# Two softmaxes of a batch: all keys and all queries in one TensorE visit each, with their spare columns in mm1's banks

## The chip, the cores and the metric

The kernel runs on one core of a Trainium2 chip. Its time is the device time of one execution in microseconds (us); a comparison takes the median of several executions. The profile of one further execution gives the start and duration of every instruction. The engines are called PE (TensorE, matmuls; PEld its weight loads), DVE (VectorE), ACT (ScalarE), POOL (GpSimd) and SP (SyncE, which issues most of the DMAs). Each takes its instructions in the order in which the program has them.

## The reference

Per batch (8) and head (8), 32 packed queries `p` attend to 576 keys and values, and then the 576 queries `q` attend to the 32 packed rows. Two feed-forward layers follow, the second with one of eight experts per token.

```python
def sm_attn(qq, kk, vv):
    s = scale * np.matmul(qq, kk.transpose(0, 1, 3, 2))
    s = s - np.max(s, axis=-1, keepdims=True)
    a = np.exp(s)
    a = a / (np.sum(a, axis=-1, keepdims=True) + 1e-09)
    return np.matmul(a, vv)
p_packed = sm_attn(p, k, v)
out = sm_attn(q, p_packed, p_packed)
...
h = x @ w_in                       # _moe_ref, 4608 tokens, 512 -> 2048 -> 512
g = h * (1.0 / (1.0 + np.exp(-h)))
return (g @ w_out).astype(np.float32)
...
e_idx = np.argmax(logits, axis=1)  # _moe2_ref, the chosen one of 8 experts
h = np.maximum(x[mask] @ w1[e], 0.0)
out[mask] = gate_w[mask, None] * eom[mask, e, None] * (h @ w2[e])
```

## The kernel before

The order of the work is written out by hand. `batch(b)` runs 16 steps f for each of the 8 batches. In a step PE does mm1 (12 matmuls of 288 columns into `ps_h`: the first feed-forward product for 128 hidden columns and the batch's 576 tokens) and then mm2 of two steps before (12 matmuls of 512 columns into four accumulators). Between them ACT applies tanh to `ps_h` (L728), DVE multiplies tanh plus one by `ps_h` into g (L729, the product), and ACT and DVE split g into a high and a low part (L734, L739; L746, L748 for the last 64 tokens). In odd batches step 1 has 48 further matmuls in mm2 at the end of the batch before.

PSUM has eight banks: four accumulators, two for `ps_h`, and two for `ps_a`, which serves everything else. There is one buffer of each, so mm1 of a step waits until the product of the step before has read `ps_h`.

Beside the steps of batch b, `extra_steps` places the attention of batch b + 1 as nine small steps s1 to s9, at a step f and a position: position 0 is behind mm1, tanh and product, position 1 behind mm2. For b of 1 to 6:

- s1(h), h of 0 and 1, at (0, 1) and (3, 1): `tiles8` multiplies half of the keys by p. It issues 8 matmuls of 64 rows by 32 columns of weights, four heads by two rows of heads, each over 288 columns of a half (L579). DVE takes the maximum (L594), ACT copies the scores to e (L595); after the second half ACT takes the exponential (L601), queued in `late` and so issued in step 4.
- s2(r) at (4, 1) and (5, 1): PE transposes e (L609), ACT copies it out.
- s3 at (7, 1): PE multiplies by the values (L627), and the same visit holds the logits of the batch before (L324). DVE normalizes into pp (L632).
- s4 at (8, 1): PE turns pp and the logits; ACT copies ppt (L642); DVE sums the logits and finds the expert (L343, then `finish`, L794 to L797).
- s5(h) at (9, 1) and (12, 1): the queries of half h times ppt (L579), DVE transposes the scores (L659) and takes the maximum.
- s6, s7, s8, s9 by half: subtract and exponential; sum, reciprocal and scaling (L671 to L675); transpose back and high part; low part. s7(0) is at (10, 1), s8(0) and s9(0) at (11, 1), s7(1) at (13, 1), s8(1) and s9(1) at (14, 1).

`step_m` (8 matmuls of 512 columns, L579 with `ps_m`) comes in steps 2, 6, 10 and 14. `place` counts the tokens of each expert for the batch before (L824, 14 or 20 small matmuls) in step 11; four blocks of rows belong to it in odd batches, five in even ones; `put` then scatters them from POOL. Loads go out on SP's queue: k1 in step 0, q0 in step 3, v1 in step 5, q1 in step 9, and p, k0, v0 of the batch after in step 13. Batch 7 has no attention beside it.

Of the kernel before, what the change touches and what calls it, by code (L numbers as in the profile page):

```python
# [84 lines left out]
class Kernel:  # L85
# [10 lines left out]
    def run(self):  # L96
# [23 lines left out]
        self.flip = False  # L120
# [432 lines left out]
    def load_att(self, b, what, dst=None):  # L553
        nc, pa = self.nc, self.pa
        n, h = what[0], int(what[1:] or 0)
        if n == "p":
            src, shape = self.i["p"][b], [128, 4, NP]
        elif n == "v":
            src, shape = self.i["v"][b, h], [128, 5, 256]
        else:  # L560
            src, shape = self.i[n][b, :, :, h * HS:h * HS + HS], [128, 4, HS]
        if what == "v1" and b > 1:
            t = self.rt.tile([128, 5, DM], F32, tag="xr", name="att_v1").rearrange("p a b -> p (a b)")[:, :1280].rearrange("p (a b) -> p a b", a=5)
# [17 lines left out]
    def att_steps(self, b):  # L581
# [4 lines left out]
        def s1(h):  # L586
# [9 lines left out]
            if h == 1:  # L596
# [56 lines left out]
        def s5(h):  # L653
# [15 lines left out]
        def s7(h):  # L669
# [4 lines left out]
            eng = nc.gpsimd if b == 1 or b == h == 0 else nc.vector  # L674
            eng.tensor_tensor(out=grp(x), in0=grp(x), in1=per_token(mx[:, 1, :]), op=ALU.mult)  # L675

        def s8(h):
            y = pa.tile([128, 2, HS], F32, tag="ea", name="y2") if b or not h else self.y_first
            nc.vector.transpose(out=y.rearrange("p a b -> p (a b)"), in_=st["x"][h].rearrange("p a b -> p (a b)"))
            nc.scalar.copy(out=self.a2[b % 2][0][:, :, h * HS:h * HS + HS], in_=y)  # L680
            st["y"][h] = y

        def s9(h):
            hi, lo = [t[:, :, h * HS:h * HS + HS] for t in self.a2[b % 2]]
# [22 lines left out]
    def mm1(self, b, f):  # L707
# [433 lines left out]
```

## Time and profile before

| | us |
|---|---|
| median of three runs | 1199.94 (1199.8 to 1200.64) |
| the profiled execution | 1199.41 |
| its span, first to last instruction | 1197.6 |
| PE busy | 1148.9 (96%) |
| DVE busy | 653.6 (55%) |
| ACT busy | 463.6 (39%) |
| batches 1 to 6 in the span | 139.75 to 674.50 |

The mean granted clock of PE is 0.988. Busy time is a mean over parts with different limits; batches 1 to 6 have to be read by themselves. In the timeline a row is a run of like instructions of one engine: start, length from the first's start to the last's end, what it is, how many, and in brackets the engine's idle time before it and what ended that. The matmuls overlap, so a length is not a price: the price of something on PE is what it adds between the start of one mm1 and the start of the next.

### The profile page before, as it was taken

Reading aid. Unit: us, or ns where it says so; the run is one execution under the profiler, and the core shown is the slowest. Engines: PE = TensorE matmul, PEld = TensorE weight load, DVE = VectorE, ACT = ScalarE, POOL = GpSimd, SP = SyncE. Lnnn points to the kernel's source line nnn. Section 1 sums busy time; section 2 is a strip of 40 time slices with the busy share of each in tenths; the row PEclk is TensorE's granted clock in tenths of the full one; section 3 lists DMA queues with packets and bytes.
Section 4 is the critical chain, followed back from the end, with each engine's and each line's share of the span. In section 5 each row is a group of like instructions: output and inputs, shape, how many; then the busy total and the mean of one; then the engine's idle time right before and its main releaser. Section 6 shows DMA issues by size and latency. Waiting matters only on the chain. (4 is left out here: it accounts for less than half of the span.)

```text
span 1197.6 us, 19835 instructions
## 1 busy us (share of the span) xinstructions
PE 1148.9 (96%) x7859; PEld 951.8 (79%) x7859; DVE 653.6 (55%) x1327; ACT 463.6 (39%) x885; POOL 170.7 (14%) x178
## 2 busy tenths in 40 slices
PE   6688999999999999999999999999999999999996
PEld 3465777877877877777877888789999998998995
DVE  6988646546656446646446656354445454454531
ACT  3343443343443343443343434234343343434331
POOL 0224300000100000100000121033121303211021
PEclk8898999999999999999999999999999999999999
DMA  9565240240241230231230153145554636445211
GB/s 330 179 201 190 70 113 24 98 95 23 69 108 26 96 95 24 85 92 37 84 96 21 38 130 92 45 141 165 171 156 130 196 100 193 132 150 167 89 58 42
DMA packets 105286, 130.28 MB, mean 109 GB/s; under 512 B 13888, under 2 KB 80640, under 8 KB 104928
## 3 DMA queue, kind: packets, MB, share of 16 engines
q1 hardware_dynamic: 97888, 108.83, 30.7%
q0 software_dynamic: 7296, 20.09, 5.1%
q8 instruction: 64, 1.05, 0.4%
q14 instruction: 38, 0.31, 0.1%
HBM read 99.19 MB, written 21.57 MB: 101 GB/s over the span
## 5 line engine op out<-in xcount | busy, mean ns | idle before, releaser
L770 PE MATMUL acc<-wo,ghi 128*128 128x512 f32 x1024 | 318.4, 392 | 0.0
L719 PE MATMUL ps_h<-a,mb 128*128 128x288 f32 x1536 | 235.4, 303 | 14.6 <-DVE g L729 8.0
L719 PEld LDWEIGHTS ps_h<-a,mb 128*128 128x128 f32 x1536 | 215.8, 192 | 40.0 <-DVE g L729 15.8
L770 PEld LDWEIGHTS acc<-wo,ghi 128*128 128x128 f32 x1024 | 192.7, 188 | 37.2
L1055 PE MATMUL pu<-xt,w 128*128 128x256 f32 (+1 forms) x1536 | 214.6, 295 | 0.2
L1055 PEld LDWEIGHTS pu<-xt,w 128*128 128x128 f32 x1536 | 208.4, 189 | 6.1 <-issue 0.8
L770 PE MATMUL acc<-wo,glo 128*128 128x512 f32 x512 | 204.4, 399 | 0.0
L1080 PE MATMUL py<-w,xt 128*128 128x512 f32 x768 | 188.2, 394 | 0.0
L1080 PEld LDWEIGHTS py<-w,xt 128*128 128x128 f32 x768 | 144.2, 188 | 33.4
L729 DVE SCALAR_TENSOR_TENSOR g<-g,ps_h 128x576 f32<-128x576 f32 x128 | 96.1, 750 | 118.2 <-ACT g L728 118.2
L1061 DVE SCALAR_TENSOR_TENSOR xt<-pu,xt 128x512 fp32r<-128x512 f32 (+1 forms) x128 | 58.7, 458 | 156.2 <-ACT xt L1060 150.2
L1060 ACT ACTIVATE xt<-pu 128x512 fp32r<-128x512 f32 (+1 forms) x128 | 52.6, 411 | 222.7 <-PE pu L1055 163.5
L728 ACT ACTIVATE g<-ps_h 128x576 f32<-128x576 f32 x128 | 83.3, 651 | 142.1 <-PE ps_h L719 134.7
L770 PEld LDWEIGHTS acc<-wo,glo 128*128 128x128 f32 x512 | 96.6, 189 | 42.8 <-issue 20.5
L739 DVE TENSOR_TENSOR glo<-g,ghi 128x512 fp32r<-128x512 f32 x128 | 91.3, 713 | 60.1 <-ACT ghi L734 59.5
L841 POOL DMA_INDIRECT perm<-pay,dsti x36 | 35.2, 979 | 575.0 <-DVE dsti L839 512.7
L734 ACT CAST ghi<-g 128x512 fp32r<-128x512 f32 x128 | 79.4, 620 | 87.8 <-DVE g L729 86.7
L1017 DVE TENSOR_TENSOR w<-raw,w 128x1024 fp32r<-128x1024 f32 x64 | 78.3, 1225 | 43.1 <-ACT w L1016 28.9
L1016 ACT CAST w<-raw 128x1024 fp32r<-128x1024 f32 x64 | 66.9, 1047 | 0.0
L700 DVE TENSOR_TENSOR mb<-ps_m,mb 128x1024 fp32r<-128x1024 f32 (+1 forms) x35 | 39.1, 1117 | 19.0 <-ACT mb L696 18.7
L770 PE MATMUL accL<-wo,gl 128*128 128x512 f32 x192 | 46.0, 394 | 0.0
L1097 POOL DMA_INDIRECT out<-y,xix x32 | 39.3, 1228 | 46.8 <-ACT y L1089 37.7
(189 smaller groups left out, 918.1 us busy)
## 6 DMA issues: line engine op xcount, KB each, us to landing
raw<-in_w SPq DMA_DIRECT2D x64, 512.0 KB
att_v<-in_v SPq DMA_DIRECT2D x15, 640.0 KB
att_k<-in_k SPq DMA_DIRECT2D x15, 576.0 KB
stg<-in_w_in SPq DMA_DIRECT2D x16, 512.0 KB
stg<-in_w_out SPq DMA_DIRECT2D x16, 512.0 KB
xr<-xr SPq DMA_DIRECT2D x32, 256.0 KB
att_q<-in_q SPq DMA_DIRECT2D x14, 576.0 KB
mid<-xr SPq DMA_DIRECT2D x28, 256.0 KB
```

The lines of the kernel that those rows point to most:

```text
L719: nc.tensor.matmul(ps[:, hf, :288], lw[:, qd, fs], rx[:, qd, ts], start=(i == 0), stop=(i == 5))
L728: nc.scalar.activation(out=g2, in_=ps[:, :, :288], func=AF.Tanh, scale=0.5)
L729: nc.vector.scalar_tensor_tensor(out=g2, in0=g2, scalar=1.0, in1=ps[:, :, :288], op0=ALU.add, op1=ALU.mult)
L734: self.nc.scalar.copy(out=hi, in_=self.graw[:, :512])
L739: self.nc.vector.tensor_tensor(out=lo, in0=self.graw[:, :512], in1=self.ghi.bitcast(F32), op=ALU.subtract)
L770: self.nc.tensor.matmul(acc, l, r, start=(first and i == 0), stop=(last and i == 2))
L1016: nc.scalar.copy(out=hi, in_=raw)
L1017: nc.vector.tensor_tensor(out=lo, in0=raw, in1=hi.bitcast(F32), op=ALU.subtract)
L1055: nc.tensor.matmul(ps[:, hf, :m], w[:, k, r, fs], xt[:, l, k, ts], start=(i == 0), stop=(i == 11))
L1060: nc.scalar.activation(out=hi, in_=src, func=AF.Relu)
L1061: nc.vector.scalar_tensor_tensor(out=lo, in0=src, scalar=0.0, in1=hi.bitcast(F32), op0=ALU.max, op1=ALU.subtract)
L1080: nc.tensor.matmul(self.acc[j], hl[:, l + j * 128:l + j * 128 + 128], w[:, r], start=(first and i == 0), stop=(last and i == 2))
```

## The change

For the attention of batches 2 to 7 s1 and s5 are replaced by s1_all and s5_all. Each does all 576 columns in one visit (`whole`): 288 columns of the first half and 224 of the second fill the two banks of `ps_a`, and the last 64 go into columns 288 to 351 of the two banks that the next mm1 uses; mm1 then takes that same tile (`next_h`). There are two new positions: -2 is ahead of mm1, -1 between mm1 and tanh. The 64-column part is read by DVE at -1 and, for s1, copied by ACT at 0.

The second softmax goes by rows of heads (one row, 576 columns) instead of halves of the columns; x takes e's buffer and y the one that x had. Exponential, s2, s4, s5 to s9, place and the loads move to other steps: exponentials to (2, 1), s2 to (3, 1) and (4, 1), s4 to (8, 0), s7(0) to (11, 0), place to (15, 0).

```diff
+            run(sched.get((f, -2), []))
             self.mm1(b, f)
             self.fill(b, 1, True)
+            run(sched.get((f, -1), []))
             self.act(b, f)
...
-                mid = ((4, 1, "s2", 0), (5, 1, "s2", 1), (7, 1, "s3", 0, 1))
+                plan = ((0, -2, "s1", 0), (0, -1, "s1", 1), (0, 0, "s1", 2), (2, 1, "s1", 3), (3, 1, "s2", 0), (4, 1, "s2", 1), (7, 1, "s3", 0, 1), (8, 0, "s4"),
+                        (9, -2, "s5", 0), (9, -1, "s5", 1), (9, 0, "s5", 2), (10, 1, "s5", 3), (10, 0, "s6", 0), (11, 0, "s7", 0), (12, 0, "s6", 1), (12, 0, "s8", 0), (13, 0, "s9", 0), (13, 1, "s7", 1), (14, 1, "s8", 1), (15, 0, "s9", 1))
+                loads = ((0, "q0"), (0, "q1"), (4, "v0"), (4, "v1"))
...
-            for what in ("p", "k0", "v0"):
+            for what in ("p", "k0", "k1"):
...
-            at(11, 0, lambda: self.place(self.group))
+            at(15 if b + 1 < B else 11, 0, lambda: self.place(self.group))
...
+        def whole(x0, x1, lhs):
+            ps = self.psum(b)
+            rest = self.next_h = self.ps_h.tile([128, 2, 512], F32, tag="h", name="ps_h")
+            self.tiles8(ps, HS, lhs, lambda r, c: x0[r, c, :])
+            self.tiles8(ps[:, :, HS:], 512 - HS, lhs, lambda r, c: x1[r, c, :512 - HS])
+            self.tiles8(rest[:, :, HS:], S - 512, lhs, lambda r, c: x1[r, c, 512 - HS:])
+            return ps, rest[:, :, HS:HS + S - 512]
+
+        def s1_all(h):
+            if h == 0:
...
+                nc.vector.tensor_reduce(out=sm[:, 0:2], in_=ps, axis=AX.X, op=ALU.max)
+                nc.scalar.copy(out=e[:, :, :512], in_=ps)
...
+            if h == 1:
+                nc.vector.tensor_reduce(out=sm[:, 2:4], in_=st["rest"], axis=AX.X, op=ALU.max)
...
+            if h == 2:
+                nc.scalar.copy(out=e[:, :, 512:], in_=st.pop("rest"))
+                return
+            for r in range(2):
+                nc.scalar.activation(out=e[:, r, :], in_=e[:, r, :], func=AF.Exp, bias=sm[:, 6 + r:7 + r], scale=SCALE, accum_out=sm[:, 8 + r:9 + r])
...
+        def s5_all(h):
+            if h == 0:
...
+                ps, rest = whole(q0, q1, lambda r, c: ppt[r, 32 * c:32 * c + 32])
+                x = pa.tile([128, 2, S], F32, tag="ea", name="x2")
+                for r in range(2):
+                    nc.vector.transpose(out=x[:, r, :512], in_=ps[:, r, :])
...
+            if h == 1:
+                rest = st.pop("rest")
+                for r in range(2):
+                    nc.vector.transpose(out=st["x"][r][:, 0, 512:], in_=rest[:, r, :])
+                return
+            h -= 2
+            mx = st["mx"][h] = pa.tile([128, 2, S // NP], F32, tag="mx", bufs=2, name="mx")
+            nc.vector.tensor_reduce(out=mx[:, 0, :], in_=grp(st["x"][h]), axis=AX.X, op=ALU.max)
...
+        return {**steps, "s1": s1_all, "s5": s5_all} if b > 1 else steps
...
-        ps = self.ps_h.tile([128, 2, 512], F32, tag="h", name="ps_h")
+        ps = self.next_h or self.ps_h.tile([128, 2, 512], F32, tag="h", name="ps_h")
+        self.next_h = None
```

The order of PE's instructions around the first visit of batch 3's attention. Before, it stands between mm2 of step 0 and mm1 of step 1 (L770 is mm2, L719 mm1, L579 the visit):

```order
L770 MATMUL acc_2330<-wo_109,glo 128x512
L770 MATMUL acc_2330<-wo_110,ghi 128x512
L770 MATMUL acc_2330<-wo_109,ghi 128x512
L579 MATMUL ps_s<-att_k,att_p 32x288 x8
L719 MATMUL ps_h<-a_911,mb 128x288
L719 MATMUL ps_h<-a_912,mb 128x288
```

Now, between mm2 of step 15 of the batch before and mm1 of step 0 (L837, L786 and L590 are the same lines in the changed kernel):

```order
L837 MATMUL acc_2364<-wo_109,glo 128x512
L837 MATMUL acc_2364<-wo_110,ghi 128x512
L837 MATMUL acc_2364<-wo_109,ghi 128x512
L590 MATMUL ps_s<-att_k,att_p 32x288 x8
L590 MATMUL ps_s<-att_k,att_p 32x224 x8
L590 MATMUL ps_h<-att_k,att_p 32x64 x8
L786 MATMUL ps_h<-a_911,mb 128x288
L786 MATMUL ps_h<-a_912,mb 128x288
```

Two further groups stand in the visit, the last of them in `ps_h`; the second visit with keys, in step 3, is gone.

ACT around the exponentials of the same attention. Before, from step 3's last split to step 5's tanh (L728 tanh, L734 and L746 splits, L595 the copy of the second half, L601 the exponentials, L615 and L616 the copies of s2):

```order
L746 CAST gl<-g 128x64
L595 COPY e_3082<-ps_s 128x2x288
L728 ACTIVATE g<-ps_h 128x576
L734 CAST ghi<-g 128x512
L746 CAST gl<-g 128x64
L601 ACTIVATE e_3082,sm<-e_3082,sm 128x576 x2
L615 COPY a1t<-ps_s 128x512
L616 COPY a1t<-ps_s 64x128
L728 ACTIVATE g<-ps_h 128x576
```

Now, from step 2's splits on (L795 tanh, L801 and L813 splits, L762 step_m's copy, L644 the exponentials, L656 and L657 the copies of s2):

```order
L795 ACTIVATE g<-ps_h 128x576
L762 CAST mb<-ps_m 128x1024
L801 CAST ghi<-g 128x512
L813 CAST gl<-g 128x64
L644 ACTIVATE e_3089,sm<-e_3089,sm 128x576 x2
L795 ACTIVATE g<-ps_h 128x576
L801 CAST ghi<-g 128x512
L813 CAST gl<-g 128x64
L656 COPY a1t<-ps_s 128x512
```

The exponentials stand in step 2 now, with the whole of step 3 between them and the copies that follow s2's transposes.

DVE from step 10's splits to step 11's in batch 3. Before (L729 the product, L671 to L675 s7(0), L829 and L830 of place, L739 and L748 splits):

```order
L748 TENSOR_TENSOR gl<-g,gl 128x64
L808 TENSOR_REDUCE rt<-sh 128x4
L809 TENSOR_SCALAR rt<-rt 128x4
L810 SCALAR_TENSOR_TENSOR rt<-sh,rt 128x4
L813 COPY pay_95<-tok 128x4
L814 RECIPROCAL pay_95<-rt 128x4
L671 TENSOR_REDUCE mx<-x_3559 128x18
L672 TENSOR_SCALAR mx<-mx 128x18
L673 RECIPROCAL mx<-mx 128x18
L675 TENSOR_TENSOR x_3559<-x_3559,mx 128x576
L729 SCALAR_TENSOR_TENSOR g<-g,ps_h 128x576
L829 TENSOR_TENSOR dst<-ps_r,nt_run 128x4x8
```

Now (L796 the product, L730 to L734 s7(0), L721 the maximum of s5_all's second row, L806 and L815 splits):

```order
L815 TENSOR_TENSOR gl<-g,gl 128x64
L721 TENSOR_REDUCE mx<-x_3574 128x18
L796 SCALAR_TENSOR_TENSOR g<-g,ps_h 128x576
L730 TENSOR_REDUCE mx<-x_3574 128x18
L731 TENSOR_SCALAR mx<-mx 128x18
L732 RECIPROCAL mx<-mx 128x18
L734 TENSOR_TENSOR x_3574<-x_3574,mx 128x576
L806 TENSOR_TENSOR glo<-g,ghi 128x512
```

s7(0) has gone from ahead of step 11's product to behind it, and the first operations of place are no longer there.

## Rows read from the trace of the kernel before

**Rows 1.** Busy time by engine in batch 2: stretch, length, each engine, clock, DMA.
```profile
223.06:317.90 94.84, 94.11 (x693) 75.19 (x692) 50.45 (x117) 37.03 (x76) 4.79 (x5) 1.00 0.25 68
```
**Rows 2.** PE's waits from 139.75 to 749.6: for what, us in total, times, longest.
```profile
PE ps_s L609 <- ACT e L601: 2.5, 6, 0.4
PE ps_h L719 <- DVE g L729: 2.5, 6, 0.5
```
**Rows 3.** PE's timeline, batch 2 step 15 to batch 3 step 3: start, length.
```profile
313.57 1.75 PE L719 MATMUL ps_h<-a,mb 128*128 128x288 f32 x12
...
317.90 1.75 PE L719 MATMUL ps_h<-a,mb 128*128 128x288 f32 x12
...
322.97 1.86 PE L719 MATMUL ps_h<-a,mb 128*128 128x288 f32 x12
...
327.42 1.75 PE L719 MATMUL ps_h<-a,mb 128*128 128x288 f32 x12
...
332.98 1.75 PE L719 MATMUL ps_h<-a,mb 128*128 128x288 f32 x12
```
**Rows 4.** PE's timeline, s3 of batch 2 and the two mm1 behind it.
```profile
275.94 0.74 PE L627 MATMUL ps_s<-att_v,a1t 128*32 128x64 f32 x40
276.50 0.74 PE L627 MATMUL ps_s<-att_v,a1u 128*32 128x64 f32 x40
277.17 1.86 PE L719 MATMUL ps_h<-a,mb 128*128 128x288 f32 x12
...
282.19 1.05 PE L719 MATMUL ps_h<-a,mb 128*128 128x288 f32 x6
```
**Rows 5.** PE's timeline, batch 3, steps 4 and 5 with the two s2.
```profile
338.05 1.85 PE L719 MATMUL ps_h<-a,mb 128*128 128x288 f32 x12
...
343.06 0.77 PE L609 MATMUL ps_s<-cst,e 128*128 128x128 f32 x5 [0.42 <-ACT e L601]
343.58 1.84 PE L719 MATMUL ps_h<-a,mb 128*128 128x288 f32 x12
...
348.47 0.77 PE L719 MATMUL ps_h<-a,mb 128*128 128x288 f32 x4
```
**Rows 6.** PE's timeline, steps 11 and 12 of batch 3, then of batch 7.
```profile
376.36 1.75 PE L719 MATMUL ps_h<-a,mb 128*128 128x288 f32 x12
...
381.79 0.40 PE L719 MATMUL ps_h<-a,mb 128*128 128x288 f32 x1 [0.48 <-DVE g L729]
...
727.47 1.75 PE L719 MATMUL ps_h<-a,mb 128*128 128x288 f32 x12
...
732.25 0.95 PE L719 MATMUL ps_h<-a,mb 128*128 128x288 f32 x6
```
**Rows 7.** DVE's timeline, batch 3 step 11, then batch 2 steps 8 and 9.
```profile
379.04 0.72 DVE L671 TENSOR_REDUCE mx<-x 128x18 f32<-128x576 f32 x1
...
380.99 0.75 DVE L729 SCALAR_TENSOR_TENSOR g<-g,ps_h 128x576 f32<-128x576 f32 x1
...
278.03 0.48 DVE L632 TENSOR_SCALAR pp<-ps_s,sm 128x64 f32<-128x64 f32 x2 [2.82 <-ACT mid L328]
279.81 0.76 DVE L729 SCALAR_TENSOR_TENSOR g<-g,ps_h 128x576 f32<-128x576 f32 x1 [1.30 <-ACT g L728]
...
282.77 0.49 DVE L343 TENSOR_REDUCE lg<-ps_s 128x80 f32<-128x320 f32 x1 [0.69 <-ACT ppt L642]
...
285.46 0.75 DVE L729 SCALAR_TENSOR_TENSOR g<-g,ps_h 128x576 f32<-128x576 f32 x1
```
**Rows 8.** DVE's groups by shape, batches 1 to 6: busy us, mean ns | idle before.
```profile
L700 DVE TENSOR_TENSOR mb<-ps_m,mb 128x1024 fp32r<-128x1024 f32 x24 | 29.4, 1224 | 14.4 <-ACT mb L696 14.1
...
L659 DVE STREAM_TRANSPOSE x<-ps_s 128x288 f32<-128x288 f32 x24 | 10.1, 457 | 0.0
```
**Rows 9.** ACT's groups by shape, batches 1 to 6.
```profile
L728 ACT ACTIVATE g<-ps_h 128x576 f32<-128x576 f32 x96 | 62.5, 651 | 101.8 <-PE ps_h L719 100.7 <-ACT gl L746 0.6
...
L696 ACT CAST mb<-ps_m 128x1024 fp32r<-128x1024 f32 x24 | 24.3, 1011 | 9.5 <-PE ps_m L579 9.5
```

More of the change, by code (lines that the diff above doesn't have):

```diff
@@ L118, in run @@
         self.tab = cp.tile([1, 3, NGRP], I32, name="tab")
-        self.flip = False
+        self.flip, self.next_h = False, None
         self.ppt, self.m, self.g, self.loads = {}, {}, {}, {}
@@ L561, in load_att @@
             src, shape = self.i[n][b, :, :, h * HS:h * HS + HS], [128, 4, HS]
-        if what == "v1" and b > 1:
-            t = self.rt.tile([128, 5, DM], F32, tag="xr", name="att_v1").rearrange("p a b -> p (a b)")[:, :1280].rearrange("p (a b) -> p a b", a=5)
+        if n == "v" and b > 1:
+            if h == 0:
+                t = self.rt.tile([128, 5, DM], F32, tag="xr", name="att_v").rearrange("p a b -> p (a b)")
+                self.values = [t[:, i * 1280:i * 1280 + 1280].rearrange("p (a b) -> p a b", a=5) for i in range(2)]
+            t = self.values[h]
+        elif n in "kq" and h and b > 1:
+            t = pa.tile([128, 5, 256], F32, tag="att_v", name=f"att_{n}").rearrange("p a b -> p (a b)")[:, :4 * HS].rearrange("p (a b) -> p a b", a=4)
         elif dst is None:
@@ L603, in s1 @@
                         scale=SCALE, accum_out=sm[:, 8 + r:9 + r]))
+        def whole(x0, x1, lhs):
[7 more added lines that the diff above has]
+            if h == 0:
+                k0, k1, p = [self.loads.pop((b, n)) for n in ("k0", "k1", "p")]
+                ps, rest = whole(k0, k1, lambda r, c: p[r, c, :])
+                sm = st["sm"] = pa.tile([128, 12], F32, tag="sm", bufs=2, name="sm")
+                e = st["e"] = pa.tile([128, 2, S], F32, tag="ea", name="e1")
+                nc.vector.tensor_reduce(out=sm[:, 0:2], in_=ps, axis=AX.X, op=ALU.max)
+                nc.scalar.copy(out=e[:, :, :512], in_=ps)
+                st["rest"] = rest
+                return
+            sm, e = st["sm"], st["e"]
+            if h == 1:
+                nc.vector.tensor_reduce(out=sm[:, 2:4], in_=st["rest"], axis=AX.X, op=ALU.max)
+                nc.vector.tensor_tensor(out=sm[:, 4:6], in0=sm[:, 0:2], in1=sm[:, 2:4], op=ALU.max)
+                nc.vector.tensor_scalar(out=sm[:, 6:8], in0=sm[:, 4:6], scalar1=-SCALE, scalar2=None, op0=ALU.mult)
+                return
+            if h == 2:
+                nc.scalar.copy(out=e[:, :, 512:], in_=st.pop("rest"))
+                return
+            for r in range(2):
+                nc.scalar.activation(out=e[:, r, :], in_=e[:, r, :], func=AF.Exp, bias=sm[:, 6 + r:7 + r], scale=SCALE, accum_out=sm[:, 8 + r:9 + r])
         def s2(r):
@@ L675, in s7, with half @@
             eng.tensor_tensor(out=grp(x), in0=grp(x), in1=per_token(mx[:, 1, :]), op=ALU.mult)
+        def half(t, h):
+            return t[:, h:h + 1, :] if b > 1 else t[:, :, h * HS:h * HS + HS]
         def s8(h):
-            y = pa.tile([128, 2, HS], F32, tag="ea", name="y2") if b or not h else self.y_first
+            if b > 1:
+                y = pa.tile([128, 2, HS], F32, tag="eb", name="y2").rearrange("p a b -> p (a b)").unsqueeze(1)
+            else:
+                y = pa.tile([128, 2, HS], F32, tag="ea", name="y2") if b or not h else self.y_first
             nc.vector.transpose(out=y.rearrange("p a b -> p (a b)"), in_=st["x"][h].rearrange("p a b -> p (a b)"))
-            nc.scalar.copy(out=self.a2[b % 2][0][:, :, h * HS:h * HS + HS], in_=y)
+            nc.scalar.copy(out=half(self.a2[b % 2][0], h), in_=y)
             st["y"][h] = y
         def s9(h):
-            hi, lo = [t[:, :, h * HS:h * HS + HS] for t in self.a2[b % 2]]
+            hi, lo = [half(t, h) for t in self.a2[b % 2]]
             eng = nc.gpsimd if b == 1 else nc.vector
             eng.tensor_tensor(out=lo, in0=st["y"][h], in1=hi.bitcast(F32), op=ALU.subtract)
-        return {f.__name__: f for f in (s1, s2, s3, s4, s5, s6, s7, s8, s9)}
+        steps = {f.__name__: f for f in (s1, s2, s3, s4, s5, s6, s7, s8, s9)}
+        return {**steps, "s1": s1_all, "s5": s5_all} if b > 1 else steps
     def step_m(self, b, c, split=False):
```

15 lines of the change are left out of this document (11 added, 4 removed).

## Prediction

> **What bounds the kernel now.** I read four views in this order. First the busy time of each engine over one whole batch: TensorE (PE) is busy 94.11 of 94.84 us at a granted clock of 1.00, DVE 50.45, ACT 37.03 [rows 1]. So a us taken out of PE's own sequence in batches 1 to 6 is a us of the run, and another engine counts only where PE stands waiting for it. Second, PE's waits in those six batches: two groups and no more, six waits for the exponential of the first softmax and six for the DVE product that frees mm1's bank [rows 2]; no wait is for a transfer. Third, PE's timeline, read from the start of one mm1 to the start of the next. A plain step (mm1 and mm2, nothing else) takes 317.90 - 313.57 = 4.33 us, and whatever a step takes beyond that is the price of what was put into it, its drain and the slower first matmul behind it included [rows 3]. Fourth, DVE's timeline at the two places where PE waits or may come to wait.
>
> The sum is made on the profiled run: 1199.41 us with a span of 1197.6. The median of the three runs, 1199.94, is 0.53 above it, and I add that at the end.
>
> **Part 1, one visit for two.** Before, s1 and s5 each come to PE twice a batch with 8 matmuls of 288 columns. Now they come once, with 288, 224 and 64 columns back to back; the 64 lie in the unused columns of mm1's two banks. Price before: the step with the visit takes 322.97 - 317.90 = 5.07 us, the one behind it 327.42 - 322.97 = 4.45, together 0.86 over two plain steps [rows 3]. The next visit, 8 matmuls of 512 columns (step_m), makes a step of 5.56, so 1.23 [rows 3]. From the two: 0.37 us for 224 columns, 1.65 ns a column, and some 0.38 for coming and going. One visit of 576 columns is then 1.23 + 64 x 1.65 ns = 1.34, against 2 x 0.86 = 1.72: 0.38 saved. Six batches have two such pairs each: 12 x 0.38 = **4.6 us**. The unseen piece is the 64-column group of 16 records. Nearest row: in s3, matmuls of 64 columns start 0.56 us apart for 40 records, 14 ns each [rows 4], so 16 of them could take 0.22 instead of 0.11, leaving 0.27 a pair, 3.2 us. At the other end they cost nothing, hidden in the drain: 0.49 a pair, 5.9 us. I take 0.11: in s3 four tiles share a pass, and four times 14 ns is just what 64 columns take in one of fp32's two passes (64 x 1.65 / 2 = 53 ns), so there, too, the columns bind.
>
> The Trainium skill, "TensorE: Matmul & The Clock Gate", section "Wait — 56ns, not 53.3ns?", says that matmuls never start less than about 25 ns apart, however few their columns; by that the group would take an estimated 0.40 us and this part would give 1.1 us instead of 4.6. The 14 ns of s3 speak against it.
>
> **Part 2, the exponential earlier.** Before, both exponentials stand on ACT behind step 4's own work, and s2(0) comes to PE at that step's end: PE waits. The step takes 343.58 - 338.05 = 5.53, the like step with s2(1) 348.47 - 343.58 = 4.89, both with a slow first matmul [rows 5]; less the 0.02 by which these differ, the wait is worth 0.62. Now the exponentials are issued in step 2 and s2(0) at the end of step 3, so the exponentials move by two steps and their reader by one: they gain a whole step, at least 4.3 us, on a wait of 0.6. The wait goes; next late would be s2's copies, wanted four steps on. 6 x 0.62 = **3.7 us**; counted by the recorded idle alone, 2.5 [rows 2].
>
> **Part 3, the normalizing behind the product.** Before, s7(0) stands on DVE ahead of step 11's product, from 379.04 to 380.99; the product then ends at 381.74 [rows 7] and mm1 of step 12 waits for it. This step takes 5.43 us; the step of batch 7 that holds the same place() but no attention takes 732.25 - 727.47 = 4.78. The wait is worth 0.65 there, with 0.48 recorded idle [rows 6]; the mean of the six is 0.42 idle [rows 2], so I take 0.59: **3.5 us** in all, 2.5 by idle alone. Now s7(0) comes behind that product, and nothing but the split for step 13 waits for it. s7(1) still stands ahead of a product, in step 14, as before, and step_m covers it there.
>
> **Part 4, moved at no price.** The place() matmuls go from step 11 to 15, the same count between the same neighbours. s1's visit waits for place()'s last DVE sum, which now follows the product and s9 of step 15; behind mm1 that makes tanh 0.65, product 0.75, s9 about as long, two small sums 0.35 and handovers 0.3, 2.8 us, while place()'s matmuls and mm2 keep PE for 0.45 + 2.8: 0.4 to spare. s4 goes from behind mm2 to directly behind mm1 of step 8: it needs pp, done at 278.51, and PE gets there some 1.7 us after 277.17, at 278.87, so 0.35 us remain [rows 4, 7]. Were that cover gone, the lack would be paid six times. The bigger loads on SP's queue have three or more steps until use, at least 13 us, past the same stores and regroupings as before; the put() scatters on POOL start four steps later, and their first reader, the index fetch of batch 7, stands behind that batch's own stores on SP's queue. Row-wise halves of x and y leave the element counts of s6 to s9 the same.
>
> **Part 5, the new waits.** Readers of one bank go one after the other: already now pp waits on DVE until ACT has copied its share of that bank. So in steps 0 and 9 the 64-column readers stand behind mm1, and tanh behind them, then the product, then (step 0) one more copy, and only then is mm1's single buffer free. Unseen lengths by slope: DVE needs 1224 ns for 1024 columns and 457 for 288 from PSUM, so about 0.69 for 512 [rows 8]. Step 9, with five blocks, on the old clock: product of step 8 over at 280.57; row sums and arg-max took 282.77 to 285.46, 2.69, so until 283.26 [rows 7]; split and first pick operations about 1.15: 284.4. The visit begins where mm1 of step 9 began, near 282.1 [rows 4], and its 512 columns are ready by 283.3, so DVE is the later one. Two wide transposes to 285.8, two narrow ones (0.2 each) to 286.2, tanh 0.65 [rows 9] to 286.9, product 0.76 to 287.65. mm1 of step 10 is due at 283.4 + 4.45 = 287.85: 0.2 us to spare, 0.6 with four blocks. Step 0, from the visit's start: columns ready 1.2, reduce to 2.4, ACT copy 1.01 [rows 9] to 3.5, tanh 4.2, product 5.0, narrow copy 5.3; due 5.7. Price taken: nothing. If the estimates are off, each visit pays what exceeds its margin.
>
> The Trainium skill, "PSUM — Partial Sum Buffer", section "Terms", says that two engines on one bank and quadrant at once collide, reads against reads included; it agrees with pp's wait and makes this chain serial by need.
>
> **Sum.** 4.6 + 3.7 + 3.5 = 11.8; 1199.41 - 11.8 = 1187.6, and with 0.53 **1188.1 us**. Lower bounds of the three: 3.2 + 2.5 + 2.5 = 8.2, 1191.7. Upper: 5.9 + 3.7 + 3.5 and 0.1 for each slow first matmul behind step 11's wait, 13.7: 1186.2.
>
> **Rivals.** *Gains paid back in the shared bank*: the chain of part 5 misses by 0.5 us at each of 12 visits, 6.0 back, 1194.1. For it: 0.2 and 0.4 us of margin rest on slopes. Against it: consecutive DVE operations overlap a little, which I didn't count. *Each matmul pays for its start*: the narrow groups are bound by issue, not columns. Even at s3's 14 ns this is 1.4 us, 1189.5; at four times 0.11 a group, 4.0 us, 1192.1. *Slower*: the wide readers, too, run behind mm1, not under it, because DVE reaches them late. Then step 0 needs 1.2 + 1.0 + 0.65 + 0.75 + 0.25 and six handovers of 0.05 to 0.06 (the product's end at 381.74 to mm1's start at 381.79 is one [rows 6, 7]), 4.2 us, where mm1's end leaves 2.6; step 9 needs 1.4 + 0.4 + 0.65 + 0.75 + 0.3 = 3.5. That is 1.6 + 0.9 = 2.5 a batch, 15 us: 1199.94 - 11.8 + 15 = 1203.1. It decides from 1.97 us a batch on. Against it: DVE would have to be 1 us later at both places than I count. *No change*: coming and going is paid by each group of 8, not by the visit, so a visit costs 3 x 0.38 + 0.95 = 2.09, 4.4 us more in all, and the waits give their recorded idle alone, 5.0: 1199.3. Against it: s3's groups follow each other without a gap [rows 4].
>
> **Chances.** Forecast 0.66 (1186.2 to 1191.7), paid back in the bank 0.15, start price beyond s3's 0.05, no change 0.06, slower 0.08. The range reaches to the bank rival: 1186.0 to 1194.1. Faster by over 0.2% (about what a measurement of this kernel can tell from none, 2.4 us) takes the first three: 0.86; same 0.06; slower 0.08.
>
> **What would show it.** Right: batches of 94.84 us [rows 1] shorter by about 1.9; PE's waits for exponential and product of step 11 gone; steps with a visit about 1.23 us over plain and 0.11 in the step behind. Wrong: PE idle before mm1 of steps 1 or 10 on an ACT copy or DVE product; s4 waiting for pp; the narrow group spreading over more than 0.2 us.

## The result and the profile after

| | before | after |
|---|---|---|
| median, us (4 runs each) | 1199.87 (1198.67 to 1200.64) | 1188.20 (1187.96 to 1188.44) |
| profiled execution, and its span | 1199.41, 1197.6 | 1188.28, 1186.4 |
| first mm1 of batch 1 to first mm1 of batch 7 | 534.75 | 521.72 |
| step 15 of batch 0, which now holds a visit | 4.34 | 5.55 |

The ratio is 0.9904, 95% interval 0.9886 to 0.9921: 11.7 us, 1.0%. In the profiles batches 1 to 6 lost 13.03 us and batch 0's last step gained 1.21, together 11.82. The forecast was 11.8.

One caution on reading totals. The start of batch 1 lay anywhere between 138.9 and 141.9 us in the 14 profiles of this study, by no order that an edit explains, while the six batches took 521.72 us in both profiles of the changed kernel. So single terms of tenths are read from the six batches, step by step (start of one mm1 to the start of the next), and the medians are given beside them.

In the kernel after, mm1 is L786, mm2 L837, the visits and step_m L590, s2 L650, place L891, the product L796. Busy time by engine of batch 2 (stretch, length, PE, PEld, DVE, ACT, POOL, clock, DMA share, GB/s), to be held against [rows 1]:

```profile
222.80:315.76 92.96, 92.96 (x736) 76.48 (x725) 50.20 (x117) 36.66 (x74) 4.30 (x5) 1.00 0.26 70
```

Batch 2 went from 94.84 to 92.96, and PE is busy all of it. The view of PE's waits, which had two lines before [rows 2], has none for these batches. PE's timeline around the first visit, batch 2 step 15 to batch 3 step 1, and around the second, batch 2 step 9:

```profile
309.60 1.74 PE L786 MATMUL ps_h<-a,mb 128*128 128x288 f32 x12
311.18 0.66 PE L891 MATMUL ps_r<-oh,tri 128*128 128x8 bf16 x20
...
314.62 1.09 PE L590 MATMUL ps_s<-att_k,att_p 64*32 64x288 f32 x32
315.51 0.32 PE L590 MATMUL ps_h<-att_k,att_p 64*32 64x64 f32 x16
315.76 1.86 PE L786 MATMUL ps_h<-a,mb 128*128 128x288 f32 x12
...
320.20 1.83 PE L786 MATMUL ps_h<-a,mb 128*128 128x288 f32 x12
```
```profile
279.94 1.09 PE L590 MATMUL ps_s<-att_q,ppt 64*32 64x288 f32 x32
...
281.07 1.86 PE L786 MATMUL ps_h<-a,mb 128*128 128x288 f32 x12
...
285.52 1.75 PE L786 MATMUL ps_h<-a,mb 128*128 128x288 f32 x12
```

The step with the visit took 315.76 - 309.60 = 6.16; batch 6, with the same 20 matmuls of place() and no visit behind, took 4.94. So the visit adds 1.22, and the step behind it takes 4.45 (285.52 - 281.07) over 4.33: 1.33 in all, forecast 1.34 [rows 3]. s2 and step 11, batch 3:

```profile
330.19 1.75 PE L786 MATMUL ps_h<-a,mb 128*128 128x288 f32 x12
334.52 0.71 PE L650 MATMUL ps_s<-cst,e 128*128 128x128 f32 x5
334.99 1.84 PE L786 MATMUL ps_h<-a,mb 128*128 128x288 f32 x12
...
339.88 1.83 PE L786 MATMUL ps_h<-a,mb 128*128 128x288 f32 x12
...
372.61 1.75 PE L786 MATMUL ps_h<-a,mb 128*128 128x288 f32 x12
...
376.94 1.75 PE L786 MATMUL ps_h<-a,mb 128*128 128x288 f32 x12
```

No row carries an idle time in brackets any more where [rows 5] and [rows 6] had one: the steps with s2 take 4.80 and 4.89, step 11 takes 4.33. The chains through the shared banks, first DVE in batch 2 step 9, then DVE, ACT and POOL in step 0 of batch 3 and of batch 4, the latter with PE's mm1 of step 1:

```profile
278.03 0.48 DVE L343 TENSOR_REDUCE lg<-ps_s 128x80 f32<-128x320 f32 x1
...
281.79 1.30 DVE L711 STREAM_TRANSPOSE x<-ps_s 128x512 f32<-128x512 f32 x2
283.01 0.34 DVE L717 STREAM_TRANSPOSE x<-ps_h 128x64 f32<-128x64 f32 x2
284.15 0.75 DVE L796 SCALAR_TENSOR_TENSOR g<-g,ps_h 128x576 f32<-128x576 f32 x1 [0.80 <-ACT g L795]
```
```profile
316.21 1.23 DVE L630 TENSOR_REDUCE sm<-ps_s 128x2 f32<-128x1024 f32 x1 [0.83 <-PE ps_h L590]
...
319.86 0.27 ACT L641 COPY e<-ps_h 128x128 f32<-128x128 f32 x1 [0.82 <-DVE g L796]
...
315.65 0.96 POOL L908 DMA_INDIRECT perm<-pay,dsti  x1 [79.92 <-DVE dsti L906]
```
```profile
397.20 1.23 DVE L630 TENSOR_REDUCE sm<-ps_s 128x2 f32<-128x1024 f32 x1 [0.34 <-PE ps_h L590]
...
400.89 0.27 ACT L641 COPY e<-ps_h 128x128 f32<-128x128 f32 x1 [0.82 <-DVE g L796]
...
401.59 1.75 PE L786 MATMUL ps_h<-a,mb 128*128 128x288 f32 x12
...
397.14 0.96 POOL L908 DMA_INDIRECT perm<-pay,dsti  x1 [68.18 <-DVE dsti L906]
```

Step 9's product ends at 284.90, 0.62 ahead of the mm1 that needs the bank (285.52). Step 0's narrow copy ends at 320.13 in batch 3, 0.07 ahead of mm1 (320.20), but at 401.16 in batch 4, 0.43 ahead of 401.59. In batch 5 it is 0.05. In these two batches, 3 and 5, mm1 of step 1 begins with a slow matmul, as behind a wait (1.83 us in batch 3 for the 1.75 of batch 4), and step 1 takes 4.43 and 4.45 where it takes 4.34 in batch 1.

### The profile page after: what moved, and what is told of

The parts are those of the page before. It is cut to its first block, busy times and chain, and to the rows that moved or that the text cites. A ratio compares the mean times of both kernels' runs of the same rounds, so it can differ in the third digit from the quotient of the medians.

```text
span 1186.4 us, 20212 instructions
## 1 busy us (share of the span) xinstructions
PE 1146.6 (97%) x8051; PEld 964.1 (81%) x8051; DVE 652.0 (55%) x1327; ACT 463.0 (39%) x885; POOL 169.5 (14%) x178
## 5 line engine op out<-in xcount | busy, mean ns | idle before, releaser
L837 PE MATMUL acc<-wo,ghi 128*128 128x512 f32 x1024 | 319.9, 394 | 0.0
L786 PE MATMUL ps_h<-a,mb 128*128 128x288 f32 x1536 | 236.3, 304 | 10.5 <-DVE mb L766 3.8
L786 PEld LDWEIGHTS ps_h<-a,mb 128*128 128x128 f32 x1536 | 220.5, 194 | 25.5 <-DVE g L796 6.0
L837 PEld LDWEIGHTS acc<-wo,ghi 128*128 128x128 f32 x1024 | 193.8, 189 | 37.7
L837 PE MATMUL acc<-wo,glo 128*128 128x512 f32 x512 | 205.8, 402 | 0.0
L796 DVE SCALAR_TENSOR_TENSOR g<-g,ps_h 128x576 f32<-128x576 f32 x128 | 96.3, 752 | 139.4 <-ACT g L795 138.0
L795 ACT ACTIVATE g<-ps_h 128x576 f32<-128x576 f32 x128 | 83.4, 652 | 164.8 <-PE ps_h L786 153.3
L837 PEld LDWEIGHTS acc<-wo,glo 128*128 128x128 f32 x512 | 97.1, 190 | 42.9 <-issue 20.5
L806 DVE TENSOR_TENSOR glo<-g,ghi 128x512 fp32r<-128x512 f32 x128 | 90.7, 708 | 42.6 <-ACT ghi L801 41.7
L801 ACT CAST ghi<-g 128x512 fp32r<-128x512 f32 x128 | 79.5, 621 | 63.6 <-DVE g L796 63.5
L837 PE MATMUL accL<-wo,gl 128*128 128x512 f32 x192 | 46.0, 394 | 0.0
```

Source lines behind the costliest of these rows:

```text
L786: nc.tensor.matmul(ps[:, hf, :288], lw[:, qd, fs], rx[:, qd, ts], start=(i == 0), stop=(i == 5))
L795: nc.scalar.activation(out=g2, in_=ps[:, :, :288], func=AF.Tanh, scale=0.5)
L796: nc.vector.scalar_tensor_tensor(out=g2, in0=g2, scalar=1.0, in1=ps[:, :, :288], op0=ALU.add, op1=ALU.mult)
L801: self.nc.scalar.copy(out=hi, in_=self.graw[:, :512])
L806: self.nc.vector.tensor_tensor(out=lo, in0=self.graw[:, :512], in1=self.ghi.bitcast(F32), op=ALU.subtract)
L837: self.nc.tensor.matmul(acc, l, r, start=(first and i == 0), stop=(last and i == 2))
```

## The experiments

### Part 3 alone, part 2 alone

```diff
-(10, 1, "s7", 0),
+((11, 0) if b else (10, 1)) + ("s7", 0),
```


> The kernel before with part 3 alone: for batches 2 to 7 s7(0) stands at (11, 0), behind the product of step 11, and nothing else is moved. My theory (each term stands alone, because only TensorE's own time and its waits count): step 11 falls from 5.43 to about 4.78 us, the wait of mm1 of step 12 for the product is gone, and the run is 3.5 to 3.9 us shorter than before, about 1196.2 us against 1199.9. Rival (the wait only moves on): DVE has the same work, s7(0) now delays the split of step 11 and the halves behind it, TensorE waits there instead, and the time stays within 1 us of before.

1195.75 us (1195.08 to 1196.9), ratio to before 0.9973, interval 0.9963 to 0.9984; six batches 531.61, so 3.14 less. PE's and DVE's timelines of batch 3, steps 11 to 13 (L719 mm1, L579 the visit, L686 s9(0), L729 the product):

```profile
374.46 1.74 PE L719 MATMUL ps_h<-a,mb 128*128 128x288 f32 x12
...
379.25 1.75 PE L719 MATMUL ps_h<-a,mb 128*128 128x288 f32 x12
...
383.67 0.72 PE L579 MATMUL ps_s<-att_q,ppt 64*32 64x288 f32 x16
384.52 1.86 PE L719 MATMUL ps_h<-a,mb 128*128 128x288 f32 x12
```
```profile
383.05 0.76 DVE L686 TENSOR_TENSOR a<-y,a 128x576 fp32r<-128x576 f32 x1 [0.74 <-ACT a L680]
383.72 0.75 DVE L729 SCALAR_TENSOR_TENSOR g<-g,ps_h 128x576 f32<-128x576 f32 x1
```

Step 11 takes 379.25 - 374.46 = 4.79 where it took 5.43; summed over the six batches it fell from 32.55 to 29.11, 3.44. But 0.29 came back in steps 12 and 13: s9(0), which follows s7(0) and s8(0) on DVE, now runs so late that the next product, behind it, ends at 384.47, and mm1 of step 13 begins 0.05 later. The rival had a grain of truth; the run with the merge undone, below, shows what made s9(0) late.

```diff
-mid = ((4, 1, "s2", 0), (5, 1, "s2", 1), (7, 1, "s3", 0, 1))
+mid = ((5, 1, "s2", 0), (6, 1, "s2", 1), (7, 1, "s3", 0, 1))
```


> The kernel before with part 2 alone, done the other way round: the exponentials stay in step 4, and the two transposing visits s2(0) and s2(1) go one step later, to (5, 1) and (6, 1). My theory: the wait for the exponential goes, step 4 falls from 5.54 to about 4.4 and step 5 keeps 4.9, together with step 6 some 0.62 to 0.65 us less a batch, so 3.7 to 3.9 us less in all, about 1196.1 us. Rival: s2(1) now stands behind step_m of step 6 in the one buffer for small things, and waits there for DVE's low part, which may end about as late as mm2; then up to all of the 0.62 a batch comes back, and the time stays at 1199 to 1200 us.

1195.24 us (1194.55 to 1195.89), ratio 0.9969, interval 0.9957 to 0.998; six batches 530.85, 3.90 less. PE's timeline, batch 3, starts of steps 5, 6 and 7:

```profile
340.38 1.75 PE L719 MATMUL ps_h<-a,mb 128*128 128x288 f32 x12
...
345.17 1.82 PE L719 MATMUL ps_h<-a,mb 128*128 128x288 f32 x12
...
351.27 1.83 PE L719 MATMUL ps_h<-a,mb 128*128 128x288 f32 x12
```

Step 5 takes 4.79 and step 6, with step_m and s2(1), 6.10, just 0.55 over a step with step_m alone, so nothing waits in step 6; step 4 fell from 5.54 to 4.44. The wait was worth 0.65 a batch.

### The merge undone for the queries

```diff
-(9, -2, "s5", 0), (9, -1, "s5", 1), (9, 0, "s5", 2), (10, 1, "s5", 3), (10, 0, "s6", 0), (11, 0, "s7", 0), (12, 0, "s6", 1), ...
+(8, 1, "s5", 0), (10, 0, "s6", 0), (11, 0, "s7", 0), (11, 1, "s8", 0), (11, 1, "s9", 0), (12, 1, "s5", 1), (13, 0, "s6", 1), ...
...
```


> The changed kernel with the merge undone for the second softmax alone: s5 comes to TensorE in two visits of 288 columns again, behind mm2 of steps 8 and 12, with halves by columns and s6 to s9 as before; s1 stays merged, s7(0) stays behind the product, place stays in step 15. My theory (coming and going is paid once a visit, 0.38 us): 6 x 0.38 = 2.3 us longer than the changed kernel, 1190.5 us; steps 8 and 12 each hold a visit of about 0.74 over plain, and the steps behind them 0.11. Rival one (each small matmul pays for its start, so that the narrow group costs 0.40): the merge saves 0.09 a visit, and this kernel is at 1188.7. Rival two (the price is paid by each group of eight matmuls): two visits cost less than one with three groups, and this kernel is faster than the changed one, under 1188.

1189.43 us (1188.54 to 1190.22); six batches 523.64, 1.92 more than the changed kernel. PE's timeline, batch 3, steps 8 to 10, 12 and 13, and DVE's in step 12 (L783 mm1, L748 s9(0), L793 the product); then the start of step 13 in the kernel before:

```profile
357.39 1.86 PE L783 MATMUL ps_h<-a,mb 128*128 128x288 f32 x12
...
363.14 1.86 PE L783 MATMUL ps_h<-a,mb 128*128 128x288 f32 x12
...
367.59 1.75 PE L783 MATMUL ps_h<-a,mb 128*128 128x288 f32 x12
...
377.48 1.75 PE L783 MATMUL ps_h<-a,mb 128*128 128x288 f32 x12
...
382.54 1.85 PE L783 MATMUL ps_h<-a,mb 128*128 128x288 f32 x12
```
```profile
380.56 0.76 DVE L748 TENSOR_TENSOR a<-y,a 128x576 fp32r<-128x576 f32 x1 [0.74 <-ACT a L742]
381.24 0.74 DVE L793 SCALAR_TENSOR_TENSOR g<-g,ps_h 128x576 f32<-128x576 f32 x1
```
```profile
386.99 1.85 PE L719 MATMUL ps_h<-a,mb 128*128 128x288 f32 x12
```

Step 8 takes 5.75 against 6.24 with the whole visit, step 9 4.45 in both, and steps 12 and 13 take 5.06 and 4.44 against 4.33 each. Over the six batches that is 2.95 less and 5.08 more: 2.13, 0.36 a pair of visits. (Step 1 gives 0.22 back: the maximum of step 0 isn't late here, see the last section.) Both rivals are out: coming and going is paid by the visit.

The run tells something of part 3, too. Its step 12 holds the same visit as step 12 of the kernel before, but takes 382.54 - 377.48 = 5.06 and not 386.99 - 381.79 = 5.20 [rows 6], 0.73 less in the six batches: with the wait of step 11 the slow first matmul behind it goes as well. And s8(0) and s9(0) stand where they stood in the run of part 3 alone, s9(0) ahead of the product, yet the product ends at 381.98, 0.56 before mm1 of step 13. What is missing between s7(0) and s8(0) are place()'s small sums, which ran from 379.75 to 381.54 there, around the split. So it is the move of place() that keeps the rest of part 3; moving s8(0) and s9(0) wasn't needed for it.

### The price of the narrow group

```diff
+            for _ in range(3):
                 self.tiles8(rest[:, :, HS:], S - 512, lhs, lambda r, c: x1[r, c, 512 - HS:])
```


> The changed kernel with the group of 8 matmuls of 64 columns issued three times in a row in each visit, so 24 such groups more in the run, each writing the same values again. My theory (columns set the price, 1.65 ns each): 24 x 0.11 = 2.6 us longer, 1190.8 us. Rival (each of the 16 records costs the 14 ns that s3's matmuls showed): 24 x 0.22 = 5.4, 1193.6 us. The rule of the Trainium skill, TensorE: Matmul & The Clock Gate, section Wait - 56ns, not 53.3ns?, of some 25 ns from start to start would make it an estimated 24 x 0.40 = 9.6, 1197.8 us.

1197.45 us (1196.97 to 1199.27), 9.3 more: my number fell, and the total looks like the 25 ns rule. The steps say otherwise. PE's timeline of the kernel with three groups, the narrow groups in batch 3 step 8, then in step 15:

```profile
365.31 0.75 PE L590 MATMUL ps_h<-att_q,ppt 64*32 64x64 f32 x48
```
```profile
400.27 0.57 PE L590 MATMUL ps_h<-att_k,att_p 64*32 64x64 f32 x31
401.07 0.32 PE L590 MATMUL ps_h<-att_k,att_p 64*32 64x64 f32 x6 [0.23 <-issue]
401.81 0.37 PE L590 MATMUL ps_h<-att_k,att_p 64*32 64x64 f32 x11 [0.41 <-issue]
```

Step 8 grew from 6.24 to 6.67 for 32 more records, 13 ns each, s3's 14 [rows 4] and not my 7. Step 15 grew by 1.58, and PE stands idle there waiting for no engine. (Step 15 of batch 0, which has a visit and no place(), grew by 0.43 alone.) Two runs took this apart.

```diff
-            rest = self.next_h = self.ps_h.tile([128, 2, 512], F32, tag="h", name="ps_h")
...
-            self.tiles8(rest[:, :, HS:], S - 512, lhs, lambda r, c: x1[r, c, 512 - HS:])
-            return ps, rest[:, :, HS:HS + S - 512]
+            return ps, ps[:, :, 448:512]
```


> The changed kernel without the group of 64 columns: each visit issues 288 and 224 columns only, and the readers of the last 64 columns read the 64 columns before them instead, from the two banks of the visit. So the scores of the last 64 keys and queries are left out; everything else, the readers' sizes too, is as in the changed kernel. It prices the first narrow group, which the threefold one could not. My theory (64 columns at 1.65 ns): 12 x 0.11 = 1.3 us less than the changed kernel's 1188.2, so 1186.9. Rival (14 ns a record): 12 x 0.22 = 2.6 less, 1185.6. At four times 0.11, which is what the further groups of the threefold kernel cost on average, 12 x 0.40 = 4.8 less, 1183.4. A gain from the bank no longer shared can't show, since TensorE waits for nothing in these batches.

PE's timeline, batch 3, starts of steps 8 and 9 (L784 mm1):

```profile
354.16 1.86 PE L784 MATMUL ps_h<-a,mb 128*128 128x288 f32 x12
...
360.29 1.86 PE L784 MATMUL ps_h<-a,mb 128*128 128x288 f32 x12
```

Step 8 is 6.13 for 6.24, step 15 of batch 3 5.89 for 6.00: the one narrow group of the change costs 0.11, 12 x 0.11 = 1.3. (The median, 1185.39, is 2.8 below 1188.2. Of that 1.6 is in the six batches and the visit ahead of them, 0.2 of it in step 1, and the rest lies before batch 1.)

```diff
-            at(15 if b + 1 < B else 11, 0, lambda: self.place(self.group))
+            at(11, 0, lambda: self.place(self.group))
```


> The kernel with the narrow group three times, with place() back in step 11. With place() in step 15, the threefold groups cost 0.43 us in step 8 but 1.58 in step 15, where the trace shows TensorE idle twice, 0.23 and 0.41 us, for nothing but the issue of its next instruction. Theory (the instructions come to TensorE at a limited rate and from a small stock, and the 14 or 20 short matmuls of place() in the same step use it up): the idle gaps go, step 15 pays 0.43 like step 8, and the run is 12 x 0.43 = 5.2 us longer than the changed kernel, 1193.4. Rival (the gaps belong to the first visit itself or to its place in the program): they stay, 1197.5.

1191.61 us (1190.94 to 1192.72); six batches 526.12, 4.40 more than the changed kernel, and 0.43 more in batch 0's step 15. In step 15 of batch 3 the 48 records now run without a gap, as in step 8:

```profile
397.65 0.75 PE L590 MATMUL ps_h<-att_k,att_p 64*32 64x64 f32 x48
```

Step 15 takes 5.98, 1.64 over plain: the visit's 1.21 and 0.43. So the gaps came with the 14 or 20 short matmuls of place() in the same step, as the theory had it. What runs short there is not seen in any row beyond the word issue.

### The margins in the shared banks

```diff
                 nc.scalar.copy(out=e[:, :, :512], in_=ps)
+                nc.scalar.copy(out=e[:, 0, :HS], in_=ps[:, 0, :HS])
...
                     nc.vector.transpose(out=x[:, r, :512], in_=ps[:, r, :])
+                nc.vector.transpose(out=x[:, 0, :HS], in_=ps[:, 0, :HS])
```


> The changed kernel with one more operation in each of the two chains through the shared banks: in step 0 ACT copies 288 columns of the wide scores a second time (about 0.41 us between the 0.27 of 128 columns and the 0.62 of 512), ahead of tanh; in step 9 DVE transposes 288 columns a second time (0.46 us), ahead of the narrow transposes. By the trace of the changed kernel, step 0's narrow copy ends 0.07 us before mm1 of step 1 begins, and step 9's product 0.62 before mm1 of step 10. Theory from that: step 0 pays 0.3 to 0.4 a batch, step 9 nothing: 6 x 0.35 = 2.1 us more, 1190.3. Rival, the margins as the prediction had them (0.4 in step 0; 0.2 and 0.6 in step 9): step 0 pays nothing, step 9 0.25 in three batches, 0.8 us in all, 1189.0.

1188.93 us (1187.93 to 1189.6); six batches 523.06, 1.34 more. PE's timeline, steps 0 and 1 of batch 3 (L788 mm1, L642 the narrow copy):

```profile
315.01 1.86 PE L788 MATMUL ps_h<-a,mb 128*128 128x288 f32 x12
...
319.89 1.32 PE L788 MATMUL ps_h<-a,mb 128*128 128x288 f32 x8 [0.27 <-ACT e L642]
```

The same 0.4 us cost 0.43 in batches 3 and 5 (step 0 takes 4.88 for 4.45), 0.02 in 2, 4 and 6, and 0.14 in batch 1, with up to 0.11 for a slow first matmul behind; step 9 paid nothing. In all six batches mm1 of step 1 now begins 0.05 us behind the narrow copy, so 0.05 is what a mm1 shows that has waited for it. Neither expectation held: mine had taken batch 3's margin for all six. By the trace of the changed kernel it is 0.43 in three batches, 0.35 in batch 1, and 0.07 and 0.05, that is next to nothing, in batches 3 and 5.

```diff
-(8, 0, "s4"),
+(8, 1, "s4"),
```


> The changed kernel with s4 alone back at (8, 1), behind mm2 of step 8 and so directly ahead of the visit with all queries. Theory: the visit then waits for ACT's copy of ppt, some 0.5 us, and DVE reaches the wide transposes only after the row sums and arg-max, about 1.5 us later than now, which is more than the 0.62 to spare, so that mm1 of step 10 waits too, by 0.2 to 0.5: 6 x 0.85 = 5 us more, 1193.3. Rival (the place of s4 doesn't matter, its matmuls cost the same in either): 1188.2.

1192.53 us (1191.83 to 1194.16); six batches 527.17, 5.45 more, nearly all of it in step 8 (7.11 and 7.29 for 6.24 and 6.35). The view of PE's waits has one line:

```profile
PE ps_s L590 <- DVE lg L343: 5.1, 6, 0.9
```

The size was as expected, the mechanism only in part. The visit doesn't wait for ppt alone: the row sums of s4 read the same single buffer, DVE takes them after ACT's copy, and only then may the visit write. And mm1 of step 10 doesn't wait (step 9 takes 4.46). With s4 ahead of mm2 all of this lies under mm2.

### Shorter than both

```diff
...
-        for r in range(n + 1):
-            for q in range(min(r + 1, n)):
-                nc.tensor.matmul(ps[:, 0, r * E8:r * E8 + E8], self.tri[:, int(q < r), :], oh[:, q, :],
-                                 start=(q == 0), stop=(q == min(r, n - 1)))
+        cols = lambda a, b: ps[:, 0, a * E8:b * E8]
+        nc.tensor.matmul(cols(0, n + 1), self.tri[:, 1, :], g["rows"][:, :n + 1, :], start=True, stop=False)
+        for k in range(2, n + 1):
+            nc.tensor.matmul(cols(k, n + 1), self.tri[:, 1, :], oh[:, :n + 1 - k, :], start=False, stop=False)
+        nc.tensor.matmul(cols(0, n), self.tri[:, 0, :], oh[:, :n, :], start=False, stop=True)
```


> The changed kernel once more, on the same chip as the three that follow, so that they have a neighbour. Its batches 1 to 6 should take 521.7 us from the first mm1 of batch 1 to the first mm1 of batch 7, as in its first profile, whatever its time before them does; 1188.2 us as a whole, within 1.

> The changed kernel with place() in fewer matmuls and the same sums: the one-hot rows lie behind a row of zeros, and one matmul with all ones over the zeros and all blocks, n - 1 more of them shifted by a block each, and one with the triangle over all blocks stand for the 14 or 20 of 8 columns: 5 for four blocks, 6 for five. In the changed kernel's trace these matmuls start 25 ns apart. Theory (they pay for their start, since each follows on the same whole array): 9 x 25 = 0.23 us less in batches 1, 3, 5 and 7, 14 x 25 = 0.35 less in 2, 4 and 6, 2.0 us in all, 1186.2. Rival (they pay for their columns, 112 and 160 before, 120 and 168 now): no gain, 1188.2.

The changed kernel again: 1187.44 us (1186.63 to 1188.12). With the short place(): 1184.59 (1183.51 to 1185.03), ratio to before 0.9882, interval 0.9866 to 0.9899; six batches 519.81, 1.91 less, and step 11 of batch 7 4.54 for 4.78. PE's timeline in step 15 of batch 2, with five blocks:

```profile
308.74 0.20 PE L894 MATMUL ps_r<-oh,tri 128*128 128x48 bf16 x1
308.78 0.24 PE L896 MATMUL ps_r<-oh,tri 128*128 128x32 bf16 x4
308.88 0.18 PE L897 MATMUL ps_r<-oh,tri 128*128 128x40 bf16 x1
308.90 0.47 PE L840 MATMUL acc<-wo,glo 128*128 128x512 f32 x1
```

Six matmuls from 308.74 to 308.90, where twenty took 311.18 to 311.70: step 15 falls by 0.35 with five blocks and by 0.22 with four. These matmuls pay for their start.

```diff
-(3, 1, "s2", 0), (4, 1, "s2", 1),
+(4, -2, "s2", 0), (4, -1, "s2", 1),
...
+                for r in range(2):
+                    for c in range(4):
+                        nc.tensor.transpose(ps[:, r, c * 128:c * 128 + 128], e[:, r, c * 128:c * 128 + 128], self.ident)
+                for r in range(2):
+                    nc.tensor.transpose(rest[:64, r, HS:HS + 128], e[:, r, 512:], self.ident)
...
```


> The kernel with the short place(), and both transposing visits s2 in one ahead of mm1 of step 4, the last 64 rows of each in mm1's spare columns, by the pattern of this change. The transposes start 109 ns apart and use the array as the large matmuls do. Theory (the 0.35 of coming and going belongs to visits that split the array into tiles; a transposing visit has only the slow first matmul behind it, 0.09): 6 x 0.09 = 0.5 us less than the short place() alone, 1185.7. Rival (every visit has 0.38): 6 x 0.38 = 2.3 less, 1183.9.

1184.43 us (1184.13 to 1185.47); six batches 519.61, 0.2 less than with the short place() alone, where 0.5 and 2.3 were expected. PE's timeline, batch 3, ahead of mm1 of step 4 (L808):

```profile
332.47 1.03 PE L668 MATMUL ps_s<-cst,e 128*128 128x128 f32 x8
...
333.48 1.83 PE L808 MATMUL ps_h<-a,mb 128*128 128x288 f32 x12
```

From 332.47 to 333.48 is 1.01, and two visits took 2 x 0.47 (334.99 - 334.52 is one). With the slow first matmul once and not twice almost nothing is left: the same merge that gave 0.36 for split-array visits gives 0.03 here.

```diff
-            at(15 if b + 1 < B else 11, 0, lambda: self.place(self.group))
+            at(11, 0, lambda: self.place(self.group))
```


> The same with place() back in step 11 for all batches. In batches 3 and 5 of the changed kernel the wide maximum of step 0 begins 1.6 us after its visit and not 1.2, with POOL's first scatter begun 0.17 us ahead of it, and step 1 is 0.1 longer. Theory (that scatter holds DVE up): with place() in step 11 the maximum begins at 1.2 in every batch, step 1 takes 4.34, and the run gains another 0.2 us, 1185.5. Rival (the place of place() is worth nothing): 1185.7 and the late maximum stays.

1184.34 us (1184.22 to 1184.52), ratio to before 0.9879, interval 0.9863 to 0.9896; six batches 519.48, another 0.13. But step 1 had been at 59.55 for the six batches already with the short place() in step 15, against 59.76 in the changed kernel; there DVE's small sums end later and POOL's scatter begins behind the maximum. So both halves of the expectation failed: the late maximum was gone beforehand. This is the fastest kernel of the study; the three short ones can't be told apart by their medians.

## Why the prediction was right

- **What bounds the kernel.** PE's own sequence was the measure: it is busy 521.72 of 521.72 us after, and every term shows where it was put.
- **Part 1, forecast 4.6.** 0.36 a pair by undoing it for the queries; for the keys 2 x 0.86 [rows 3] less 1.33 is 0.39, or 0.37 with the 4.34 that a plain step 1 takes in batch 7. So some 4.4. The narrow group costs the 0.11 taken. Whether its columns bind, as I had it, is not shown: its 16 records cost 7 ns each, and eight of these make the same 53 ns as 64 columns in one pass. Further groups cost 13 ns a record, near the other end of the range.
- **Part 2, forecast 3.7:** 3.9 alone. **Part 3, forecast 3.5:** 3.44 at step 11 and 0.73 at step 12, for the slow first matmul behind the wait, which the prediction has in its upper bound alone: 4.2. Done alone it gives 3.14, and the prediction didn't see that it needs the move of place() for the rest.
- **Sum.** Measured apart, the terms make 4.4 + 3.9 + 4.2 = 12.5; together they gave 11.82. Of the difference 0.2 is lost in step 1 of batches 3 and 5, and the rest are tenths that I don't divide further. The mechanism held, but that 11.8 was met to a few hundredths is luck: part 1 gave 0.2 less than forecast, parts 2 and 3 gave 0.9 more, and 0.7 went where the sum had nothing. The medians alone allow 9.5 to 13.7.
- **Part 4.** place() costs the same in step 15 with five blocks (6.15 less the 5.55 of a step with the visit alone, 0.60) as in step 11 (4.92 less 4.33, 0.59, with the threefold groups). s4 never waits for pp; its move was worth far more than the "no price" at which I put it, since without it each batch pays 0.9.
- **Part 5.** Taken at nothing, and it cost 0.2. The row sums of step 9 begin where the prediction had them: 278.03 is 280.48 on the old clock, counted from mm1 of step 8, for the 280.57 of the sum. But step 9 has 0.62 to spare and not 0.2, since DVE's operations overlap a little, which the prediction named and didn't count: the wide transposes begin 0.16 sooner than reckoned and the product ends 0.30 sooner, while mm1 of step 10 comes 0.12 later. Step 0 has the 0.43 that I reckoned (0.4) in three batches and 0.35 in batch 1, but next to nothing in batches 3 and 5, where the wide maximum begins 0.4 late (last section). That wasn't in the sum.
- **Rivals.** Little was paid back in the bank: 0.1 in step 1 of each of two batches. A price for each group of eight is ruled out by the queries' two visits. The rule of 25 ns (the Trainium skill, "TensorE: Matmul & The Clock Gate", section "Wait — 56ns, not 53.3ns?") does hold for matmuls on the whole array: place()'s twenty start 26 ns apart, and fewer of them saved just that. It doesn't hold for tiles: 16 records in 0.11 us are 7 ns each. The same page's section "The mechanism" puts starts on different tiles at about 4 ns; the prediction should have read that one.

## What to carry to other kernels

A visit that splits the array into tiles costs about 0.36 us here beyond its columns, so merge those, into spare columns of another bank if need be; merging two visits of transposes on the whole array gave 0.03, and many tiny matmuls there should rather become few wide ones. Where a wait is removed by moving an operation, follow its successors on the same engine to the next product. And read a margin in every batch: what runs beside it differs, and here it was 0.43 us in three batches and next to nothing in two.

## What the runs showed of the hardware

- **Bursts of tiny matmuls.** 16 records of 64 columns behind 32 wider ones cost 7 ns each (0.11 us), the next 32 cost 13 (0.43 us); with 14 or 20 short matmuls earlier in the same step PE stood idle for 0.23 and 0.41 us with no engine to wait for. The Trainium skill, "Advanced Engine Details and Errata", section "Engine Queue Depths", gives TensorE a queue of 64, "complicated with tiling". That would fit in kind; no run here measures a depth.
- **POOL ahead of DVE.** Seven profiles have the visit with all keys and the long place() in step 15. In batches 1, 2, 4 and 6 the wide maximum of step 0 began 1.20 us after the visit's start in all of them. In batches 3 and 5 of six of them POOL's scatter began 1.02 or 1.03 us after the visit's start, and the maximum at 1.59 to 1.63 (visit 314.62, scatter 315.65, maximum 316.21 in the rows above). In the seventh, with the queries apart, the scatter began at 1.07 and the maximum at 1.20; and so it did where the scatter came later or stood elsewhere. The scatter's start is the only difference found, and with it the end of the DVE sum that releases it, 0.05 later in the seventh; maxima with a still earlier last sum and no scatter came on time. Whether the scatter holds DVE up, and how, is not shown, and DVE didn't wait for its end at 316.61. The Trainium skill, "SBUF — State Buffer", section "Terms", has DVE and GpSimd share a pair of ports under a lock held for the full instruction; the delay of 0.4 us is less than the 0.96 of this one, so it isn't a wait of that length.
